# Attention scores on TensorE: the high-by-high products on 64 array rows each, the score columns over two banks, another order of steps

## The chip, the cores and the metric

The program runs on one core of a Trainium2 chip. The core has five instruction streams that wait for each other by semaphores: PE (TensorE, matrix multiply), DVE (VectorE), ACT (ScalarE), POOL (GpSimd) and SP, which here only issues DMAs. The metric is the device time of one execution in microseconds (us). The result of a matrix multiply goes to PSUM, which has 8 banks of 512 fp32 numbers in each of 128 partitions; everything else lies in SBUF.

## The reference

```python
def _attn_ref(q, k, v):                  # q, k, v: (2, 8, 576, 64) fp32
    scores = (1 / sqrt(64)) * matmul(q, k.transpose(0, 1, 3, 2))
    kth = np.partition(scores, -32, axis=-1)[..., -32:-31]
    scores = np.where(scores >= kth, scores, -1e9)
    attn = exp(scores - max(scores)); attn /= attn.sum(-1) + 1e-9
    return matmul(attn, v)

def _moe_ref(x, domain_probs, w1, w2):   # x: (1152, 512); w1: (4, 512, 1024); w2: (4, 1024, 512)
    p = domain_probs / (domain_probs.sum(-1, keepdims=True) + 1e-9)
    for e in range(4):
        out += p[:, e:e + 1] * (np.maximum(x @ w1[e], 0) @ w2[e])
```

The attention output of the 8 heads of one sequence position, side by side, is a row of x; every row goes through all four experts.

## The kernel before

**Tiles and units.** The 1152 positions are cut into ten tiles: for each of the two batches four of 128 positions and one of 64. The first tile in the program is a 64-row one (batch 0), computed in fp32; the last is the other 64-row one. A unit is one head of a 128-row tile, or a pair of heads of a 64-row tile. There are 72 units: 4, then 64 of full width (8 tiles by 8 heads), then 4.

**Numbers in two halves.** Outside the first tile every fp32 operand of a matrix multiply is split into two fp16 numbers, hi and lo. `split` does it: ACT scales, ACT writes hi, and POOL (mode "a") or DVE (mode "d") subtracts to get lo. Keys `kt[h]`, values `vt[h]`, queries, the weights of the experts, the attention weights and the hidden layer are all held so. A key tile `kt[h]` has 128 partitions: the 64 dimensions of one half, then the 64 of the other; it is made by one transposing DMA. For the queries there are two tiles: `ta` (name `qa` in rows) with the hi half on partitions 0 to 63 and lo on 64 to 127, and `tb` (`qb`) with the halves swapped.

**A unit's steps.** `emit_qk` computes scores of 128 positions by 576 keys into a PSUM tile `ps0` (two of them, each two banks). Eight DVE passes of `topk_op` (MAX8 and MATCH_REPLACE8, four rounds) find the 32 largest; ACT takes the exponential (`emit_exp`), `emit_mask` sets what is below the 32nd to zero (on DVE, or on ACT and POOL, by a letter of `MASKS`), `emit_a` splits it, `emit_at` transposes it by DMA, `emit_av` multiplies by the values on PE.

**Scores of a full unit before.** For each half of the keys (288 columns, one bank each) PE multiplies `ta` by the key tile and then `tb` by it, both with all 128 array rows: hi by hi and lo by lo, then lo by hi and hi by lo. Four matmuls of 288 columns.

```python
for j, src in enumerate((ta, tb)):
    PE.matmul(ps[:, 0:288], lhsT=src[:, x, :],
              rhs=kt[x].rearrange("p c n -> p (c n)")[:, ks], start=(j == 0), stop=(j == 1))
```

**The experts.** When the 8 units of a tile are done, its x is split and transposed (`xt`), and `m1` (three products of hi and lo, 128 columns each for a full tile), `h_hi`, `h_lo`, `m2` (512 columns each) and `evac` run for each expert and half. The eight weight arrays are split in the first fifth of the program (`w_split`, modes `W_MODE`).

**Order.** Each engine runs its instructions in program order. The order of all steps, and of the parts of a step between its `yield`s, is a table of numbers (`ISSUE`), one entry per step. Letters in strings (`H_LO`, `MASKS`, `NB`, `X_LO`, `W_MODE`, `EVAC`, `KV1`, `V0`) say for each step which engine does it.

Of the kernel before, what the change touches and what calls it, by code (L numbers as in the profile page):

```python
# [7 lines left out]
F32 = mybir.dt.float32  # L8
# [10 lines left out]
NEG = -3.0e38  # L19
# [24 lines left out]
H_LO = ('ddpp', 'ppppppdp', 'pdpdppdp', 'ppppppdp', 'pppppppp', 'pppppppp', 'pppppppp', 'pppppppp', 'pppppppp', 'pppp')  # L44

MASKS = 'ddddddddddddddddddddrrrrrrrrrrrrrrdrrrrrrrddrdrrrrrrrrrrrrrrrrrrrrrrrrrr'
NB = 'aaaapdpdddapaaaapdpdddddddpdddapppdaappaappaappaaaaapppaapaapaapppaappaa'

X_LO = 'pppdpppppp'
Q_LO = 'pppppppppp'  # L50

W_MODE = 'aaaaaaaaadaaaaaaaaaaaaaaaaadaaaa'

EVAC = ('dddp', 'dppp', 'ddpd', 'dddp', 'dppp', 'dpdp', 'dddd', 'dddd', 'dddd', 'dddd')
KV1 = dict(k='aadaaaaa', v='aaaaaaaa')
# [5 lines left out]
V0 = 'aaaaaaaa'  # L61
# [169 lines left out]
def attn_moe_kernel(tc, q, k, v, probs, w1, w2, out):  # L231
# [56 lines left out]
    with tc.manual_schedule(engines={getattr(mybir.EngineType, x) for x in MANUAL}):  # L288
# [74 lines left out]
        def prep_q(t, steps):  # L363
# [43 lines left out]
            at(steps[2], q_lo)  # L407
            at(steps[3], q_swap)

        def split(hi, lo, raw, s, mode):  # L410
            if mode == "a":
                ACT.activation(raw, raw, AF.Copy, scale=s)
            yield
# [782 lines left out]
```

## Time and profile before

| what | value |
|---|---|
| runs (3), median, lowest to highest | 553.38 us, 552.89 to 556.65 us |
| the profiled execution | 551.35 us |
| its span, first to last instruction | 549.5 us |
| mean granted TensorE clock | 0.961 |
| busy: PE, DVE, ACT, POOL | 507.8, 438.1, 372.3, 365.0 us |

The profile is of one execution; 1.85 us of it lie outside the span, and it is 2.03 us under the median of the three runs. A PE row's duration is that of one matmul from its start until its last result, and the matmuls overlap; so what a matmul costs PE is read from the distance between the starts of two rows, not from their durations. In the names of PE rows, 128\*128 or 64\*128 is how many array rows by array columns the matmul uses.

### The profile page before, as it was taken

The numbers are of one execution on the slowest core, as the hardware profiler recorded it, in microseconds if no ns is written. First come the engines' busy times: TensorE is split into PE (matmuls) and PEld (weight loads), VectorE is DVE, ScalarE is ACT, GpSimd is POOL, SyncE is SP. The second block draws the span as 40 slices with busy tenths as digits, with TensorE's granted clock in tenths as the row PEclk, the third lists the DMA queues.
The fourth block names the chain that finished last, engine by engine and source line by source line (L and its number), as shares of the span: only waits on it lengthen the run. The fifth ranks groups of instructions, "written<-read, shape, count | busy, mean of one in ns | idle before, by whom it ended". The sixth has DMA issues, their size and how long they took to land. (4 is left out here: it accounts for less than half of the span.)

```text
span 549.5 us, 16260 instructions
## 1 busy us (share of the span) xinstructions
PE 507.8 (92%) x6666; PEld 381.6 (69%) x6666; DVE 438.1 (80%) x961; ACT 372.3 (68%) x643; POOL 365.0 (66%) x410
## 2 busy tenths in 40 slices
PE   4987564889999999999999999999999999999996
PEld 2666463577777668687777678777767778676684
DVE  2899999999999999999999989999998676600101
ACT  2899999988656867787968577757766465433121
POOL 0379999989667766676979686877768273643220
PEclk9778787899999999999999999999999999999999
DMA  7999897551561362547544453362143221201100
GB/s 180 364 267 280 211 242 218 131 88 29 102 130 42 78 141 60 107 108 143 113 88 108 77 110 67 94 94 56 42 78 70 63 46 45 63 21 23 32 4 30
DMA packets 142699, 58.35 MB, mean 106 GB/s; under 512 B 130081, under 2 KB 134305, under 8 KB 142625
## 3 DMA queue, kind: packets, MB, share of 16 engines
q1 hardware_dynamic: 139200, 54.43, 43.8%
q10 hardware_dynamic: 3424, 2.88, 1.7%
q8 instruction: 52, 0.85, 0.7%
q14 instruction: 23, 0.18, 0.1%
HBM read 25.45 MB, written 2.36 MB: 51 GB/s over the span
## 5 line engine op out<-in xcount | busy, mean ns | idle before, releaser
L883 PE MATMUL m<-xt,w 128*128 128x128 f16 (+1 forms) x1280 | 200.1, 215 | 0.0
L924 PE MATMUL m<-w,h 128*128 128x512 f16 (+1 forms) x960 | 199.2, 384 | 0.0
L881 PE MATMUL m<-xt,w 128*128 128x128 f16 (+1 forms) x1120 | 178.4, 215 | 0.0
L882 PE MATMUL m<-xt,w 128*128 128x128 f16 (+1 forms) x1120 | 178.4, 215 | 0.0
L655 DVE MAX8 m<-w 128x8 f32<-128x576 f32 x216 | 161.1, 753 | 3.0
L924 PEld LDWEIGHTS <-h 128*128 128x128 f16 (+1 forms) x960 | 83.8, 102 | 89.6 <-issue 3.4
L906 POOL TENSOR_TENSOR h<-hf,h 128x512 f16<-128x512 f32 x65 | 75.3, 1159 | 75.0 <-ACT hf L899 74.2
L883 PEld LDWEIGHTS <-w 128*128 128x128 f16 x1280 | 123.8, 99 | 0.0
L881 PEld LDWEIGHTS <-w 128*128 128x128 f16 x1120 | 108.2, 98 | 3.9 <-issue 1.7
L882 PEld LDWEIGHTS <-w 128*128 128x128 f16 x1120 | 108.0, 98 | 2.3 <-issue 0.3
L659 DVE MATCH_REPLACE8 w<-m,w 128x576 f32<-128x576 f32 x144 | 106.8, 742 | 0.0
L699 ACT ACTIVATE w<-ps,nb,es 128x576 f32<-128x576 f32 x68 | 56.4, 829 | 46.8 <-DVE m L655 39.7
L726 POOL TENSOR_TENSOR a<-w,a 128x512 f16<-128x512 f32 x68 | 78.9, 1161 | 12.4 <-ACT a L724 8.4
L716 POOL TENSOR_TENSOR w<-w,d 128x576 f32<-128x576 f32 x48 | 61.4, 1281 | 36.0 <-ACT d L713 27.9
L892 ACT ACTIVATE h<-m 128x512 f16<-128x512 f32 x72 | 42.5, 591 | 53.7 <-PE m L883 48.0
L655 DVE MAX8 m<-ps 128x8 f32<-128x576 f32 x72 | 54.6, 759 | 24.7 <-PE ps L598 11.2
L948 DVE SCALAR_TENSOR_TENSOR o<-m,pniw,o 128x512 f32<-128x512 f32 (+1 forms) x17 | 12.7, 746 | 65.9 <-PE m L924 51.7
L724 ACT ACTIVATE a<-w 128x576 f16<-128x576 f32 x68 | 46.1, 680 | 15.8 <-POOL w L716 11.6
L642 PE MATMUL ps<-kt,qa 128*128 128x288 f16 x128 | 35.7, 298 | 19.8 <-DVE w L706 18.2
L657 DVE MATCH_REPLACE8 w<-m,ps 128x576 f32<-128x576 f32 x72 | 53.8, 747 | 0.0
L899 ACT ACTIVATE hf<-m 128x512 f32<-128x512 f32 x65 | 38.6, 594 | 7.0 <-POOL h L906 6.0
L764 PEld LDWEIGHTS <-at 128*128 128x128 f16 (+1 forms) x1008 | 36.6, 100 | 7.5 <-issue 1.7
(160 smaller groups left out, 786.0 us busy)
## 6 DMA issues: line engine op xcount, KB each, us to landing
w<-in_moe_w_dram SPq DMA_DIRECT2D x16, 1024.0 KB, 7.9
qraw<-in_q_dram SPq DMA_DIRECT2D x8, 256.0 KB, 3.1
qb<-qa SPq DMA_DIRECT2D x16, 128.0 KB, 2.4
out_dram<-o ACTq DMA_DIRECT2D x8, 256.0 KB, 2.2
at<-a SPq DMA_TRANSPOSE x68, 2.9
vraw<-in_v_dram SPq DMA_DIRECT2D x2, 512.0 KB, 8.2
nraw<-in_v_dram SPq DMA_DIRECT2D x4, 256.0 KB, 2.9
kraw<-in_k_dram SPq DMA_DIRECT2D x4, 256.0 KB, 2.8
```

The lines of the kernel that those rows point to most:

```text
L655: DVE.max(m, s_t[u] if r == 0 else w_t[u])
L657: DVE.match_replace(rows2(w_t[u]), m, s_t[u], NEG)
L659: DVE.match_replace(w_t[u], m, w_t[u], NEG)
L699: ACT.activation(rows2(w_t[u]), s_t[u], AF.Exp, bias=nb, scale=es)
L716: POOL.tensor_tensor(w, w, g, op=OP.mult)
L724: ACT.activation(a[:, 0:576], w, AF.Copy)
L726: POOL.tensor_tensor(a[:, 640:1152], w[:, 0:512], a[:, 0:512], op=OP.subtract)
L881: PE.matmul(o, lhsT=HI[e, 0, c][:, fc], rhs=xs(0, c), start=(c == 0), stop=False)
L882: PE.matmul(o, lhsT=HI[e, 0, c][:, fc], rhs=xs(1, c), start=False, stop=False)
L883: PE.matmul(o, lhsT=LO[e, 0, c][:, fc], rhs=xs(0, c), start=False, stop=(c == 3))
L906: POOL.tensor_tensor(h[:, 1], hf, h[:, 0], op=OP.subtract)
L924: PE.matmul(y[z * 64:z * 64 + M, :], lhsT=h_t[es, qd][:, p // 2, h0:h0 + M], rhs=w, start=(fc == 0 and p == 0), stop=(fc == 7 and p == 2))
```

## The change

For the 64 full units, the hi by hi product now uses 64 array rows: one matmul on rows 0 to 63 (from `ta`) for keys 0 to 255, one on rows 64 to 127 (from `tb`) for keys 256 to 575. For this the key tile holds hi on partitions 0 to 63 for the first two chunks of 128 keys, and on 64 to 127 for the other three. Then two matmuls with all 128 rows add lo by hi and hi by lo, `tb` for the first keys and `ta` for the others. The lo by lo product is left out. A unit still has four matmuls, now of 256, 320, 256 and 320 columns. The 576 score columns lie side by side, 256 at the end of one bank and 320 at the start of the next, so other engines read them as one run of 576 instead of two of 288. The split of the keys works on two parts where it had one (`KC`). Three loads of keys that stood in a fixed place ahead of the table now have places in it. `ISSUE` is another table, and the letters are other letters.

```diff
-H_LO = ('ddpp', 'ppppppdp', 'pdpdppdp', 'ppppppdp', 'pppppppp', ...
-MASKS = 'ddddddddddddddddddddrrrrrrrrrrrrrrrdrrrrrrrddrdrrrrrrrrrrrrrrrrrrrrrrrrr'
-X_LO = 'pppdpppppp'
+H_LO = ('pddd', 'ppppppdp', 'ddppppdd', 'ppdppppp', 'pdpppdpp', ...
+MASKS = 'ddddddddddddddddddddrrrrrrrrrrrrrrrrrrrrdrrrrrrrrrrrrrrrrrrrrrrrrrrrrrrr'
+X_LO = 'pppppppppp'
...
-W_MODE = 'aaaaaaaaadaaaaaaaaaaaaaaaaadaaaa'
-EVAC = ('dddp', 'dppp', 'ddpd', 'dddp', 'dppp', 'dpdp', 'dddd', ...
-KV1 = dict(k='aadaaaaa', v='aaaaaaaa')
+W_MODE = 'daaadaaaaaaaaaaaaaaaaaaaaaaaaaaa'
+EVAC = ('ddpp', 'dpdp', 'dppd', 'dppp', 'dppd', 'dppd', 'dddd', ...
+KV1 = dict(k='aaaaaaaa', v='aaaaaaaa')
...
-V0 = 'aaaaaaaa'
+V0 = 'aaaaadda'
...
 ISSUE = [
-    (41,), (57,), (3, 5), (1, 4), (29, 30), (32, 45), (22, 28), (11,), (17, 20), (21, 23, 42, 158), (44, 59, 91, 109),
...
+        KC = slice(0, 2), slice(2, 5)
+        def k_parts(hl, lo):
+            return [hl[:, c, D:2 * D] if lo != i else hl[:, c, 0:D] for i, c in enumerate(KC)]
...
-            return ps_s.tile([128, 2, 512], F32, tag="s", name="ps0")
+            return ps_s.tile([128, 1024], F32, tag="s", name="ps0")
...
+        HALF = (slice(256, 512), slice(0, 256)), (slice(512, 832), slice(256, 576))
...
-                else:
-                    for j, src in enumerate((ta, tb)):
-                        PE.matmul(ps[:, 0:288], lhsT=src[:, x, :],
-                                  rhs=kt[x].rearrange("p c n -> p (c n)")[:, ks], start=(j == 0), stop=(j == 1))
+            kf = flat(kt[x])
+            for (o, ks), src, z in zip(HALF, (ta, tb), (slice(0, 64), slice(64, 128))):
+                PE.matmul(p[:, o], lhsT=src[z, x, :], rhs=kf[z, ks], start=True, stop=False)
+            for (o, ks), src in zip(HALF, (tb, ta)):
+                PE.matmul(p[:, o], lhsT=src[:, x, :], rhs=kf[:, ks], start=False, stop=True)
...
-        for z in range(2):
-            SP.dma_start(out=kraw0[0:64, 4, :, z, :], in_=k[0, 4 * z:4 * z + 4, 512:576, :].rearrange("h p d -> p h d"))
-        load_k0(SP, 1)
         load_k0(ACT, 2)
-        load_k0(SP, 3)
...
+        at(-200, load_k0_end)
+        at(-199, load_k0, SP, 1)
+        at(-198, load_k0, SP, 3)
```

**PE, the scores of one full unit** (the second head of a tile; `ps0` is the score tile, `kt1` its key tile, `qa` and `qb` the two query tiles; LDWEIGHTS loads the stationary operand). Before:

```order
L642 LDWEIGHTS qa_1491
L642 MATMUL ps0_2474<-kt1_132,qa_1491 128x288
L642 LDWEIGHTS qb_1608
L642 MATMUL ps0_2474<-kt1_132,qb_1608 128x288
L642 LDWEIGHTS qa_1491
L642 MATMUL ps0_2474<-kt1_132,qa_1491 128x288
```

The same unit of the change, with the last matmul ahead of it and the first behind it:

```order
L893 MATMUL m1_2453<-xt_1932,w20_127 128x128
L651 LDWEIGHTS qa_1662
L651 MATMUL ps0_2507<-kt1_132,qa_1662 128x256
L651 LDWEIGHTS qb_2246
L651 MATMUL ps0_2507<-kt1_132,qb_2246 128x320
L653 LDWEIGHTS qb_2246
L653 MATMUL ps0_2507<-kt1_132,qb_2246 128x256
L653 LDWEIGHTS qa_1662
L653 MATMUL ps0_2507<-kt1_132,qa_1662 128x320
L891 LDWEIGHTS w11_126
```

The two matmuls of line 651 use 64 array rows; what stands ahead of them and behind them uses 128, so every full unit enters that form once and leaves it once.

**PE, the start of the program** (`ident` is the identity that transposes; `kraw0` and `qraw` are the loaded keys and queries; `ps0` the first scores). Before:

```order
L579 MATMUL m1_185<-ident_111,kraw0_150 128x128 x4
L579 MATMUL m2_186<-ident_111,kraw0_150 128x64
L558 MATMUL m1_196<-ident_111,qraw_155 128x64 x4
L598 MATMUL ps0_206<-kf_201,qf_204 64x288 x4
L1022 LDWEIGHTS kraw0_150
```

In the change:

```order
L571 MATMUL m1_177<-ident_111,qraw_155 128x64 x4
L592 MATMUL m1_186<-ident_111,kraw0_150 128x128 x4
L592 MATMUL m2_187<-ident_111,kraw0_150 128x64
L609 MATMUL ps0_196<-kf_193,qf_184 64x256 x2
L609 MATMUL ps0_196<-kf_193,qf_184 64x320 x2
```

The queries are transposed ahead of the keys instead of behind them.

**PE, where the second tile's experts begin** (`xt_1938` before and `xt_1932` now is that tile's transposed x; `m1` of the first tile reads `xt_917`; `m2` of the first tile reads `h`). Before:

```order
L882 LDWEIGHTS w30_1123
L882 MATMUL m1_1836<-xt_917,w30_1123 128x64
L883 LDWEIGHTS w30_1123
L883 MATMUL m1_1836<-xt_917,w30_1123 128x64
L881 LDWEIGHTS wx0_129
L881 MATMUL m1_1940<-xt_1938,wx0_129 128x128
```

In the change:

```order
L774 MATMUL av_1901<-vt1_140,at_1653 128x65
L934 LDWEIGHTS h_1132
L934 MATMUL m2_1591<-w01_124,h_1132 64x512
L934 MATMUL m2_1591<-w11_126,h_1132 64x512
L891 LDWEIGHTS wx0_129
L891 MATMUL m1_1966<-xt_1932,wx0_129 128x128
```

The 24 matmuls of the first tile's `m2` for experts 0 and 1, second half (of which two stand here), have moved behind its `m1` of experts 2 and 3, to the place just ahead of the second tile's first `m1`.

## Rows read from the trace of the kernel before

**Rows 1.** Page, part 1: busy us, share of span, instructions.

```profile
PE 507.8 (92%) x6666; PEld 381.6 (69%) x6666; DVE 438.1 (80%) x961; ACT 372.3 (68%) x643; POOL 365.0 (66%) x410
```

**Rows 2.** Stages of the span: busy us and count by engine, granted clock, DMA.

```profile
60.00:118.00 58.00, 40.88 (x716) 32.14 (x714) 57.69 (x142) 57.03 (x78) 57.30 (x47) 0.85 0.74 163
118.00:121.50 3.50, 1.19 (x23) 1.12 (x20) 3.50 (x4) 3.19 (x5) 3.50 (x4) 0.98 0.48 132
121.50:125.00 3.50, 3.50 (x35) 3.44 (x33) 3.46 (x5) 1.86 (x2) 1.19 (x2) 0.53 0.37 84
140.00:440.00 300.00, 298.69 (x3753) 225.66 (x3752) 278.65 (x593) 213.69 (x391) 214.28 (x262) 1.00 0.44 89
440.00:545.00 105.00, 104.56 (x1517) 75.30 (x1515) 33.25 (x65) 38.92 (x67) 43.12 (x46) 1.00 0.14 33
```

**Rows 3.** Waits of PE, 118 to 545 us: total, times, longest.

```profile
PE m L881 <- DMA xt<-xhl: 2.3, 1, 2.3
PE ps L642 <- ACT d L709: 1.3, 2, 0.7
```

**Rows 4.** Full units' score matmuls (line 642) before and after 118 us.

```profile
0.00:118.00 118.00, 10.88 (x52) 0.84 0.86 224
118.00:545.00 427.00, 33.39 (x204) 1.00 0.36 74
```

**Rows 5.** Timeline, PE, a full unit's scores at 395 us: start, duration, instruction.

```profile
394.74 0.59 PE L924 MATMUL m<-w,h 128*128 128x512 f16 x2
395.18 0.29 PE L642 MATMUL ps<-kt,qa 128*128 128x288 f16 x1
...
395.54 0.29 PE L642 MATMUL ps<-kt,qb 128*128 128x288 f16 x1
395.67 0.22 PE L881 MATMUL m<-xt,w 128*128 128x128 f16 x1
```

**Rows 6.** Timeline, PE, a 64-position unit's scores on 64 array columns, 444 us.

```profile
443.63 0.81 PE L924 MATMUL m<-w,h 128*128 128x512 f16 x3
444.38 0.31 PE L638 MATMUL ps<-kt,qa 128*64 128x288 f16 x2
444.52 0.29 PE L638 MATMUL ps<-kt,qb 128*64 128x288 f16 x2
...
444.77 0.29 PE L638 MATMUL ps<-kt,qb 128*64 128x288 f16 x2
444.99 0.23 PE L881 MATMUL m<-xt,w 128*128 128x128 f16 x1
```

**Rows 7.** Timeline, PE, fp32 transposes on 128, then 64 array rows, 14 us.

```profile
14.19 0.64 PE L579 MATMUL m<-ident,kraw 128*128 128x128 f32 x4
14.55 0.47 PE L579 MATMUL m<-ident,kraw 128*128 128x128 f32 x2
14.75 0.27 PE L579 MATMUL m<-ident,kraw 64*128 64x64 f32 x1
```

**Rows 8.** Timeline, the first scores: PE, ACT, DVE.

```profile
7.25 0.34 PE L579 MATMUL m<-ident,kraw 64*128 64x64 f32 x1 [0.78 <-DMA kraw<-in_k_dram]
8.51 2.19 PE L598 MATMUL ps<-kf,qf 64*64 64x288 f32 x8 [0.47 <-ACT qf L562]
10.74 0.77 DVE L655 MAX8 m<-ps 128x8 f32<-128x576 f32 x1 [8.95 <-PE ps L598]
```

**Rows 9.** Groups by line and form: busy, mean ns of one.

```profile
L420 DVE SCALAR_TENSOR_TENSOR w<-w,ws,w 128x1024 f16<-128x1024 f32 x1 | 2.2, 2224 | 0.0
L420 DVE SCALAR_TENSOR_TENSOR kraw<-kraw,kps,kt 128x320 f16<-128x320 f32 x1 | 0.5, 545 | 0.0
L573 ACT ACTIVATE kf<-m 128x64 f32<-128x64 f32 x4 | 0.9, 220 | 0.5 <-PE m L579 0.5
L728 POOL TENSOR_TENSOR a<-w,a 128x64 f16<-128x64 f32 x68 | 22.4, 331 | 0.1
```

More of the change, by code (lines that the diff above doesn't have):

```diff
@@ L43 @@
 MANUAL = ('PE', 'DVE', 'Activation', 'Pool', 'SP')
-H_LO = ('ddpp', 'ppppppdp', 'pdpdppdp', 'ppppppdp', 'pppppppp', 'pppppppp', 'pppppppp', 'pppppppp', 'pppppppp', 'pppp')
-MASKS = 'ddddddddddddddddddddrrrrrrrrrrrrrrdrrrrrrrddrdrrrrrrrrrrrrrrrrrrrrrrrrrr'
-NB = 'aaaapdpdddapaaaapdpdddddddpdddapppdaappaappaappaaaaapppaapaapaapppaappaa'
-X_LO = 'pppdpppppp'
+H_LO = ('pddd', 'ppppppdp', 'ddppppdd', 'ppdppppp', 'pdpppdpp', 'pppppppd', 'pppppppp', 'pppppppp', 'pdpppppp', 'pppp')
+MASKS = 'ddddddddddddddddddddrrrrrrrrrrrrrrrrrrrrdrrrrrrrrrrrrrrrrrrrrrrrrrrrrrrr'
+NB = 'aaaaadpadaddaddaddpddddddadpppadapppaappapaaapapaappaaaaaaapapappapaaaap'
+X_LO = 'pppppppppp'
 Q_LO = 'pppppppppp'
-W_MODE = 'aaaaaaaaadaaaaaaaaaaaaaaaaadaaaa'
-EVAC = ('dddp', 'dppp', 'ddpd', 'dddp', 'dppp', 'dpdp', 'dddd', 'dddd', 'dddd', 'dddd')
-KV1 = dict(k='aadaaaaa', v='aaaaaaaa')
+W_MODE = 'daaadaaaaaaaaaaaaaaaaaaaaaaaaaaa'
+EVAC = ('ddpp', 'dpdp', 'dppd', 'dppp', 'dppd', 'dppd', 'dddd', 'dddd', 'dddd', 'dddd')
+KV1 = dict(k='aaaaaaaa', v='aaaaaaaa')
 F32E = ()
@@ L408, in prep_q, with split @@
             at(steps[3], q_swap)
-        def split(hi, lo, raw, s, mode):
+        def split(hi, lo, raw, s, mode, parts=(slice(None),)):
             if mode == "a":
@@ L414, in split @@
             hi = hi()
-            ACT.activation(hi, raw, AF.Copy, scale=1.0 if mode == "a" else s)
+            for i, c in enumerate(parts):
+                ACT.activation(hi[i] if len(parts) > 1 else hi, raw[:, c], AF.Copy, scale=1.0 if mode == "a" else s)
             yield
-            if mode == "a":
-                POOL.tensor_tensor(lo, raw, hi, op=OP.subtract)
-            else:
-                DVE.scalar_tensor_tensor(lo, raw, s, hi, op0=OP.mult, op1=OP.subtract)
+            for i, c in enumerate(parts):
+                l, g = (lo[i], hi[i]) if len(parts) > 1 else (lo, hi)
+                if mode == "a":
+                    POOL.tensor_tensor(l, raw[:, c], g, op=OP.subtract)
+                else:
+                    DVE.scalar_tensor_tensor(l, raw[:, c], s, g, op0=OP.mult, op1=OP.subtract)
+        KC = slice(0, 2), slice(2, 5)
+        def k_parts(hl, lo):
+            return [hl[:, c, D:2 * D] if lo != i else hl[:, c, 0:D] for i, c in enumerate(KC)]
         def flat(ap):
@@ L446, in finish @@
                 hl = raw(h).bitcast(F16)
-                tmp = kt[h].rearrange("p c n -> p (c n)")[:, 0:320].rearrange("p (c d) -> p c d", d=D)
-                yield from split(lambda: tmp, hl[:, :, 0:D], raw(h), st["s"][:, hs.index(h):hs.index(h) + 1], mode[h])
+                t0 = kt[h][:, 0:2, :]
+                t1 = flat(kt[h])[:, 256:448].rearrange("p (c d) -> p c d", d=D)
+                yield from split(lambda: [t0[:, :, 0:D], t1], [t0[:, :, D:2 * D], hl[:, 2:5, 0:D]], raw(h),
+                                 st["s"][:, hs.index(h):hs.index(h) + 1], mode[h], KC)
                 yield
-                ACT.activation(hl[:, :, D:2 * D], tmp, AF.Copy)
+                ACT.activation(hl[:, 0:2, :], t0, AF.Copy)
+                ACT.activation(hl[:, 2:5, D:2 * D], t1, AF.Copy)
                 yield
@@ L550, in attn_moe_kernel @@
         s_t, w_t, m_t, a_t, at_t, av_t = {}, {}, {}, {}, {}, {}
-        HS = S // 2
         qF, kF = [None], {}
@@ L585, in scores @@
         def scores():
-            return ps_s.tile([128, 2, 512], F32, tag="s", name="ps0")
-        def rows2(w):
-            return w.rearrange("p (t n) -> p t n", t=2)
+            return ps_s.tile([128, 1024], F32, tag="s", name="ps0")
+        HALF = (slice(256, 512), slice(0, 256)), (slice(512, 832), slice(256, 576))
         def emit_qk_whole(u, x):
             p = scores()
-            s_t[u] = p[:, :, 0:HS]
-            for hf in range(2):
-                ps = p[:, hf, :]
+            s_t[u] = p[:, 256:832]
+            for o, ks in HALF:
                 for z in (slice(0, 64), slice(64, 128)):
-                    PE.matmul(ps[z, 0:288], lhsT=qF[0][z, x * 64:x * 64 + 64], rhs=kF[x][z, hf * 288:hf * 288 + 288],
-                              start=True, stop=True)
+                    PE.matmul(p[z, o], lhsT=qF[0][z, x * 64:x * 64 + 64], rhs=kF[x][z, ks], start=True, stop=True)
         def emit_a_whole(u):
@@ L630, in emit_qk @@
             p = scores()
-            s_t[u] = p[:, :, 0:HS]
-            for hf in range(2):
-                ps = p[:, hf, :]
-                ks = slice(hf * 288, hf * 288 + 288)
-                if t[2] == 64:
+            s_t[u] = p[:, 256:832]
+            if t[2] == 64:
+                for o, ks in HALF:
                     for j, src in enumerate((ta, tb)):
                         for z, h in enumerate(hpair(x)):
-                            PE.matmul(ps[z * 64:z * 64 + 64, 0:288], lhsT=src[:, x, z * 64:z * 64 + 64],
-                                      rhs=kt[h].rearrange("p c n -> p (c n)")[:, ks], start=(j == 0), stop=(j == 1))
-                else:
-                    for j, src in enumerate((ta, tb)):
-                        PE.matmul(ps[:, 0:288], lhsT=src[:, x, :],
-                                  rhs=kt[x].rearrange("p c n -> p (c n)")[:, ks], start=(j == 0), stop=(j == 1))
+                            PE.matmul(p[z * 64:z * 64 + 64, o], lhsT=src[:, x, z * 64:z * 64 + 64],
+                                      rhs=flat(kt[h])[:, ks], start=(j == 0), stop=(j == 1))
+                return
+            kf = flat(kt[x])
[3 more added lines that the diff above has]
+                PE.matmul(p[:, o], lhsT=src[:, x, :], rhs=kf[:, ks], start=False, stop=True)
         def topk_op(u, o):
@@ L656, in topk_op @@
             elif r == 0:
-                DVE.match_replace(rows2(w_t[u]), m, s_t[u], NEG)
+                DVE.match_replace(w_t[u], m, s_t[u], NEG)
             else:
@@ L698, in emit_exp @@
             es, nb = eb_t.pop(u)
-            ACT.activation(rows2(w_t[u]), s_t[u], AF.Exp, bias=nb, scale=es)
+            ACT.activation(w_t[u], s_t[u], AF.Exp, bias=nb, scale=es)
         def emit_mask(u):
             thr = m_t[u][:, 31:32]
-            w = rows2(w_t[u])
+            w = w_t[u]
             s = s_t.pop(u)
@@ L708, in emit_mask @@
                 d = sp_.tile([128, S], F32, tag="s", name="d")
-                ACT.activation(rows2(d), s, AF.Relu, bias=thr, scale=-1.0)
+                ACT.activation(d, s, AF.Relu, bias=thr, scale=-1.0)
             yield
             if MASKS[u] == "r":
-                g = d.bitcast(F16).rearrange("p (t n) -> p t n", t=2)[:, :, 0:HS]
-                ACT.activation(g, rows2(d), AF.Exp, scale=-1.0e18)
+                g = d.bitcast(F16)[:, 0:S]
+                ACT.activation(g, d, AF.Exp, scale=-1.0e18)
             yield
@@ L979, in attn_moe_kernel, with load_k0_end @@
         load_q(tiles[0])
-        for z in range(2):
-            SP.dma_start(out=kraw0[0:64, 4, :, z, :], in_=k[0, 4 * z:4 * z + 4, 512:576, :].rearrange("h p d -> p h d"))
-        load_k0(SP, 1)
         load_k0(ACT, 2)
-        load_k0(SP, 3)
+        def load_k0_end():
+            for z in range(2):
+                SP.dma_start(out=kraw0[0:64, 4, :, z, :],
+                             in_=k[0, 4 * z:4 * z + 4, 512:576, :].rearrange("h p d -> p h d"))
+        at(-200, load_k0_end)
+        at(-199, load_k0, SP, 1)
+        at(-198, load_k0, SP, 3)
         def load_v0(h0):
@@ L1045, in kv_finish @@
                 hl = khl0[:, h]
-                yield from split(lambda: hl[:, :, D:2 * D], hl[:, :, 0:D], kraw0[:, :, h % 4, h // 4], st["s"], K0[h])
+                yield from split(lambda: k_parts(hl, 0), k_parts(hl, 1), kraw0[:, :, h % 4, h // 4], st["s"], K0[h], KC)
                 yield
```

320 rows, old and new, of the table ISSUE are left out of this document.

## The prediction

> **What bounds the kernel now.** I read the shares by engine first: PE is busy 92% of the span [rows 1]. That average hides two regimes, so the stages come next [rows 2]. From 60 to 118 us DVE, ACT and POOL are all busy for 57.0 to 57.7 of 58 us and PE for 40.9: there the first units and the splits of the weights set the pace. From 140 to 440 us PE is busy 298.7 of 300 us while DVE has 278.7 and ACT and POOL some 214, and from 440 to 545 us PE has 104.6 of 105 with the others nearly idle. A busy PE need not be PE at its rate, so the waits of PE were read as the third view: from 118 to 545 us it waits 2.3 us in one place, for the second tile's transposed x, and 1.3 us in two others [rows 3]. So for 427 us PE issues matmuls without a gap, and whatever a matmul there costs or saves goes into the end of the program one for one. Ahead of 118 us it does not: there PE waits anyway. The full units' scores have 52 matmuls before 118 us and 204 after it [rows 4]; at four a unit these are 13 and 51 units. The 51 decide.
>
> **The score matmuls, what they save.** Among matmuls that use the whole array, four of 288 columns start at 395.18 us and the next work starts at 395.67 [rows 5]: 0.49 us, or 0.1225 us for 288 columns. The changed unit has 256, 320, 256 and 320 columns, the same 1152. Only if the two 64-row matmuls run beside each other does PE stream 320 columns for both, and 256 fall out: 256/288 x 0.1225 = 0.109 us a unit. No row of before has two 64-row matmuls over the same columns. The nearest are pairs that use 64 columns each: the four pairs of a 64-position unit start at 444.38, 444.52 and so on to 444.77 [rows 6], so two matmuls of 288 columns take the time of one. I take the overlap as given and keep its absence as a rival.
>
> **What they cost.** The same rows show what it costs to enter and leave such a form. Three 512-column matmuls start from 443.63; at 288 columns in 0.1225 us one takes 0.217, so the next was due at 443.63 + 3 x 0.217 = 444.28. The first pair starts at 444.38: 0.10 us late. The second pair follows after 0.14 instead of 0.12: 0.02. The last pair starts at 444.77 and the whole-array matmul behind it at 444.99, 0.22 later where 0.12 would do: 0.10. One visit to the form costs 0.22 us as these rounded rows have it, 0.20 to 0.22 in all. That is for 64 columns; for 64 rows there is one clean place [rows 7]. Four fp32 transposes on the whole array start within 0.64 - 0.27 = 0.37 us of 14.19, 0.12 us apart. The fourth starts at 14.55, and the one on 64 rows at 14.75: 0.20 us, so at least 0.08 us late. Leaving is not clean there, because the next transpose is of another chain of keys. I take 0.21 for a visit, from the 64-column row, whose matmuls are of the same kind. Lower end: 0.08 us each way, 0.16. Upper end: 0.22, and no overlap.
>
> So a full unit changes by 0.21 - 0.109 = +0.10 us, between +0.05 and +0.11 with overlap, and by +0.21 without. Over 51 units: **+5.1 us**, between +2.6 and +5.6, and +10.7 without overlap. Nothing hides it: PE has 3.6 us of waits in the whole region, and 2.3 of them are for x. The 13 early units pay it beside DVE and are free.
>
> **The start.** Before, the queries' transposes stand behind a key chunk that PE waits 0.78 us for, and the first scores wait 0.47 us more for the copied queries [rows 8]. Now they stand ahead of the keys, and the copy is done in time. The keys' second copy (0.22 us, [rows 9]) follows the chunk's transpose, which ends at 7.59, so the scores can start at about 7.85 in place of 8.51: DVE begins 0.65 us earlier. Against that, DVE has two weight splits of 2.2 us and two value splits of 0.55 us within the first 118 us [rows 9], where it had one weight split there and one behind; one `h_lo` of like size goes the other way. DVE's sum up to the second half of the second tile's x is larger by 0 to 2.6 us, by where these steps stand, while POOL loses as much. Since all three engines are full there [rows 2], I put the start at +0.1 us, ends -0.7 and +2.
>
> **The clock.** After the wait for x, during which PE was busy 1.2 of 3.5 us, the granted clock is 0.53 for 3.5 us, nearly its lower level of 1.2 of 2.4 GHz, although PE is full [rows 2]: 3.5 x 0.47 = 1.6 us of PE's time, in the region that decides. The change puts 24 matmuls of 512 columns, in pairs, just ahead of that place: 12 x 0.217 = 2.6 us of work where PE stood. If PE no longer stands, the clock may stay up. That is even odds: -0.8 us, ends -1.6 and 0. The wait itself isn't saved by this, since the same matmuls ran earlier before, in gaps.
>
> **Edits that cost nothing.** The key splits have 24 more ACT instructions and 16 more POOL ones, each a short one of at most 0.22 and 0.33 us [rows 9], so at most 5.3 us on each engine; three masks move from DVE to ACT and POOL, six `h_lo` the other way, and two evacuations. In the region that decides ACT and POOL have some 86 us free in 300 and DVE 21 [rows 2]; that covers all of it. Reading 576 columns in one run instead of two of 288 changes no count of elements. The three freed loads of keys stand in SP's queue where they stood, behind the first queries and ahead of the weights. The last units and the last tile's experts stand in nearly the same order, so the tail keeps its length.
>
> **The sum.** +5.1 + 0.1 - 0.8 = +4.4 us. The profiled execution took 551.35 us (span 549.5 and 1.85 around it); one like it would take 555.75. The median of the three runs is 2.03 us higher, and so I say 553.38 + 4.4 = **557.8 us**. A difference of about 1% (5.5 us) is what a measurement of this kernel can tell from none; this forecast lies under it.
>
> **Rivals.**
> *Entering the form is free.* If a 64-row matmul needs no pause among whole-array ones, each unit saves the whole 0.109 us: 51 x 0.109 = 5.6, with the clock and the start 6.3, so 547.1 us, and faster. Against it are rows 6 and 7: each change of form there has its 0.08 to 0.10 us, the one of 64 rows too. For it: two of those three are changes of columns, not rows, and the third is a single place. The Trainium skill ("TensorE: Matmul & The Clock Gate", the part on packing small matmuls) describes this outcome: a group of packed tiles lasts one matmul plus some 4 ns a tile, with weights loaded beside matmuls on other rows, and no price for entering. By that rule this rival's time holds; rows 6 agree with the few ns inside a pair and not with a free entry.
> *The halves don't run beside each other.* Then PE streams all 1152 columns and pays the visits as well: +10.7 - 0.8 + 0.1 = +10.0, 563.4 us, slower. It decides if the second 64-row matmul starts 0.11 us behind the first instead of some ns. For it: no such pair is in the trace. Against it: rows 6, and the two halves write different banks. The Trainium skill ("TensorEngine Tiling (Array Packing)", Gotcha 1) says that row tiles cannot write the same PSUM bank at once; by it these two may overlap. No row here shows it.
> *The new order wins back what PE loses.* If the region in which PE is full begins 4 us earlier, because its work starts earlier beside the splits, the result is 553.4 us, no change. For it: PE stands idle for 17 of 58 us before 118 us [rows 2], and every step was placed anew. Against it: the amount of DVE's work that x of the second tile needs has not shrunk.
>
> **Chances and range.** Forecast 0.56, free entry 0.16, no overlap 0.12, won back by the order 0.12, and 0.04 for what I have not thought of. The forecast's own ends are 553.7 (+2.6 - 0.7 - 1.6 = +0.3) and 561.0 (+5.6 + 2.0). The range reaches from 547.0, about the middle of the free entry, to 562.0, just under the middle of the third case: it leaves out some 0.08 on each side. Faster by over 1% is under 547.85: most of the free entry, 0.13. Slower by over 1% is over 558.9: the third case and about 0.16 of the forecast's 0.56, together 0.28. The rest, 0.59, is within 1%.
>
> **What would show it.** Where a full unit follows whole-array work, the first 64-row matmul starts about 0.10 us later than the columns ahead of it need; the second starts within 0.02 us of it; and the next whole-array matmul starts about 0.23 us behind (320 columns are 0.136, and the exit 0.10). From first start to the next work a unit takes about 0.50 us instead of 0.49, with 0.10 more ahead of it. PE's waits from 118 us on stay at 2 to 4 us, the granted clock just behind the second tile's first `m1` tells of the 1.6 us, and DVE's first MAX8 starts near 10.1 instead of 10.74. The prediction is wrong if units come without the pauses, if the pair comes one after the other, or if PE fills at another time than near 120 us.

## The result, and the profile after

The changed kernel takes 559.76 us in the median of four runs (559.21 to 560.12), the kernel before 553.23 us (552.89 to 556.65): a ratio of 1.0103, with an interval of 1.0062 to 1.0144. That is 6.5 us slower. In a second set of runs the ratio was 1.0132 (1.0098 to 1.0165), and the kernel before against itself gave 0.9998 (0.9974 to 1.0022), so the loss is real and lies at the edge of 1%. The forecast was 557.8 us. The two profiled executions differ by more than the medians, 559.7 us (span 557.9) against 551.35, because the kernel before's lies 1.9 us under its median.

The page's first part and the stages, which answer to [rows 1, 2] (busy us and count by engine, granted clock, DMA):

```profile
PE 517.1 (93%) x6666; PEld 379.8 (68%) x6666; DVE 435.9 (78%) x962; ACT 378.2 (68%) x671; POOL 365.6 (66%) x422
```

```profile
60.00:118.00 58.00, 38.32 (x608) 31.33 (x608) 56.09 (x139) 54.69 (x73) 54.34 (x45) 0.78 0.77 163
118.00:121.50 3.50, 2.73 (x92) 2.60 (x88) 3.46 (x11) 3.15 (x5) 3.44 (x3) 1.00 0.53 118
121.50:125.00 3.50, 3.50 (x42) 1.95 (x40) 3.50 (x9) 3.50 (x6) 3.50 (x3) 1.00 0.33 75
125.00:140.00 15.00, 14.54 (x197) 10.67 (x196) 14.90 (x37) 13.62 (x21) 14.13 (x11) 1.00 0.21 37
140.00:440.00 300.00, 299.32 (x3713) 217.38 (x3711) 276.21 (x586) 218.72 (x411) 219.74 (x274) 1.00 0.45 90
```

Two things differ. From 60 to 118 us DVE has 1.9 us of idle time where it had 0.3, and ACT and POOL 3.3 and 3.7 us where they had 1.0 and 0.7: the region in which they set the pace is no longer full. And the granted clock from 121.5 to 125 us is 1.00 where it was 0.53; it stays at 1.00 behind that.

PE's waits from 118 us on, answering to [rows 3], and the second tile's first `m1`, in the kernel before and now:

```profile
PE ps L651 <- DVE w L716: 0.8, 1, 0.8
PE m L891 <- DVE h L912: 0.5, 1, 0.5
PE m L891 <- DMA xt<-xhl: 0.4, 1, 0.4
PE ps L651 <- ACT d L719: 0.2, 1, 0.2
```

```profile
120.41 0.22 PE L881 MATMUL m<-xt,wx 128*128 128x128 f16 x1 [2.31 <-DMA xt<-xhl]
125.67 0.23 PE L891 MATMUL m<-xt,wx 128*128 128x128 f16 x1 [0.46 <-DVE h L912]
```

From this matmul on PE is nearly full in both. So the difference between the two traces splits at this row: the start is 5.3 us longer, and what follows it, 432.2 us in place of 429.1 (the "rest" below), is 3.1 us longer.

A full unit among whole-array work (timeline, PE), answering to [rows 5]:

```profile
395.79 1.04 PE L774 MATMUL av<-vt,at 128*128 128x65 f16 x28
396.77 0.28 PE L651 MATMUL ps<-kt,qa 64*128 64x256 f16 x1
396.77 0.31 PE L651 MATMUL ps<-kt,qb 64*128 64x320 f16 x1
397.01 0.28 PE L653 MATMUL ps<-kt,qb 128*128 128x256 f16 x1
397.13 0.30 PE L653 MATMUL ps<-kt,qa 128*128 128x320 f16 x1
397.27 2.10 PE L934 MATMUL m<-w,h 128*128 128x512 f16 x9
```

The two 64-row matmuls start in the same hundredth: they do run beside each other. The last of the 28 matmuls of 65 columns starts at 396.64 and needs 0.03 us, so the pair comes 0.10 us late; the next matmul is 0.24 us behind it. First start to next work is 0.50 us, and 0.10 more stands ahead: each number is that of the prediction.

The weight loads say more about these two pauses than the prediction did. In the kernel before, the second matmul of the unit of [rows 5] starts at 395.30 us, and its weight load at 395.18, with the matmul ahead of it. In the unit above, the load for the matmul at 396.77 starts at 396.77, and the load for the one at 397.01 at 397.01. At both edges of all 51 units the load starts with its own matmul. A load lasts 0.09 to 0.10 us, which is the size of a pause. So a load that no earlier matmul covers would account for it; no run here tells that from another cause of the same size.

The start. DVE's first MAX8 comes 0.35 us earlier than in [rows 8] (forecast 0.65; the last key chunk is transposed at 7.89 us, not at 7.25), and DVE's waits from 10 us on are these:

```profile
10.39 0.77 DVE L665 MAX8 m<-ps 128x8 f32<-128x576 f32 x1 [8.60 <-PE ps L609]
```

```profile
DVE m L665 <- PE ps L609: 10.0, 3, 8.6
DVE m L518 <- PE m L512: 3.6, 1, 3.6
DVE m L665 <- PE ps L653: 1.8, 2, 1.4
DVE wpt L282 <- PE m L521: 1.3, 1, 1.3
```

Line 512 is the sum of squares (the gram) of the third weight matrix, `w_gram` for (0, 1), line 518 its diagonal on DVE, line 521 its total on PE. The kernel before (lines 498 and 507) waits 0.7 and 0.4 us for all such:

```profile
DVE m L504 <- PE m L498: 0.7, 1, 0.7
DVE wpt L281 <- PE m L507: 0.4, 2, 0.2
```

On PE the new order has an attention product of the first tile (lines 629 and 632, unit 2) ahead of that gram and one (unit 3) ahead of its total:

```profile
42.32 1.12 PE L629 MATMUL av<-vraw,at 128*64 128x64 f32 x16
...
45.03 3.59 PE L512 MATMUL m<-w 128*128 128x128 bf16 x32
48.56 1.12 PE L629 MATMUL av<-vraw,at 128*64 128x64 f32 x16
...
51.28 0.59 PE L521 MATMUL m<-gd,ones 128*128 128x1 f32 x2
```

```profile
43.74 1.41 DVE L665 MAX8 m<-w 128x8 f32<-128x576 f32 x2
48.74 0.30 DVE L518 SCALAR_TENSOR_TENSOR m<-m,ident 128x128 f32<-128x128 f32 x1 [3.59 <-PE m L512]
```

DVE comes to the diagonal at 45.15 us, when the gram has just begun, and stands in order, with top-k work queued behind. PE has no gap there, but it is slow:

```profile
40.00:44.00 4.00, 3.82 (x37) 2.88 (x37) 4.00 (x11) 4.00 (x9) 2.71 (x5) 0.60 1.05 394
44.00:48.00 4.00, 4.00 (x48) 3.97 (x47) 1.15 (x2) 3.06 (x4) 2.24 (x4) 0.50 0.92 200
48.00:52.00 4.00, 4.00 (x51) 3.54 (x50) 1.94 (x7) 1.78 (x3) 1.27 (x1) 0.50 0.77 191
```

The granted clock of these three stretches is 0.60, 0.50 and 0.50, where 0.50 is the lower level of 1.2 GHz. In the kernel before it is 0.86, 0.72 and 1.00, and its gram takes 2.42 us, not 3.59:

```profile
45.32 2.42 PE L498 MATMUL m<-w 128*128 128x128 bf16 x32
```

```profile
40.00:44.00 4.00, 2.25 (x32) 1.92 (x31) 3.68 (x10) 4.00 (x7) 3.34 (x5) 0.86 0.40 66
44.00:48.00 4.00, 4.00 (x49) 3.33 (x49) 4.00 (x9) 3.99 (x7) 3.92 (x4) 0.72 0.98 311
48.00:52.00 4.00, 4.00 (x90) 3.57 (x85) 3.45 (x11) 3.71 (x6) 3.42 (x3) 1.00 1.15 309
```

### The profile page after: what moved, and what is told of

It reads as the page before. It is cut to its first block, busy times and chain, and to the rows that moved or that the text cites. A ratio compares the mean times of both kernels' runs of the same rounds, so it can differ in the third digit from the quotient of the medians.

```text
span 557.9 us, 16250 instructions
## 1 busy us (share of the span) xinstructions
PE 517.1 (93%) x6666; PEld 379.8 (68%) x6666; DVE 435.9 (78%) x962; ACT 378.2 (68%) x671; POOL 365.6 (66%) x422
## 4 chain that ended last, share of the span: by engine, by line
PE 71%; DVE 18%; POOL 4%; DMA 3%; issue 3%; ACT 1%; SPq 0%; POOLq 0%; DVEq 0%
PE m L934 29%; PE m L891 9%; PE m L893 9%; PE m L892 9%; DVE m L665 7%; PE av L774 4%; DVE w L669 4%; PE ps L653 3%; DVE w L667 2%; PE ps L651 2%; DVE w L716 2%; DMA at<-a 1%; PE ps L609 1%; DMA xt<-xhl 1%; DMA kraw<-in_k_dram 1%
## 5 line engine op out<-in xcount | busy, mean ns | idle before, releaser
L934 PE MATMUL m<-w,h 128*128 128x512 f16 (+1 forms) x960 | 196.7, 379 | 0.0
L916 POOL TENSOR_TENSOR h<-hf,h 128x512 f16<-128x512 f32 x59 | 68.5, 1161 | 66.6 <-ACT hf L909 66.6
L726 POOL TENSOR_TENSOR w<-w,d 128x576 f32<-128x576 f32 x51 | 65.4, 1283 | 28.2 <-ACT d L723 28.1
L958 DVE SCALAR_TENSOR_TENSOR o<-m,pniw,o 128x512 f32<-128x512 f32 (+1 forms) x15 | 11.2, 745 | 63.8 <-PE m L934 49.8
L774 PEld LDWEIGHTS <-at 128*128 128x128 f16 (+1 forms) x1008 | 38.2, 101 | 13.7 <-DMA at<-a 6.6
L774 PE MATMUL av<-vt,at 128*128 128x65 f16 (+1 forms) x1008 | 41.1, 196 | 6.1 <-DVE w L716 4.6
L719 ACT ACTIVATE d<-ps,m 128x576 f32<-128x576 f32 x51 | 37.5, 737 | 3.8 <-DMA at<-a 2.2
```

The costliest lines, as they stand in the source:

```text
L726: POOL.tensor_tensor(w, w, g, op=OP.mult)
L774: PE.matmul(o, lhsT=att[:, blk, ps], rhs=r, start=(i == 0), stop=(i == len(seq) - 1))
L916: POOL.tensor_tensor(h[:, 1], hf, h[:, 0], op=OP.subtract)
L934: PE.matmul(y[z * 64:z * 64 + M, :], lhsT=h_t[es, qd][:, p // 2, h0:h0 + M], rhs=w, start=(fc == 0 and p == 0), stop=(fc == 7 and p == 2))
```

## The experiments

Theory A was that form and order each have a cost of their own; theory B that the form costs all, C that the order does. All ratios are to the kernel before in the same set of runs; e1 to e4 are one set, the two kernels again with e5 and e6 a second, e7 to e9 a third.

**e1, the changed kernel without the 64-row form.**

```diff
-            for (o, ks), src, z in zip(HALF, (ta, tb), (slice(0, 64), slice(64, 128))):
-                PE.matmul(p[:, o], lhsT=src[z, x, :], rhs=kf[z, ks], start=True, stop=False)
-            for (o, ks), src in zip(HALF, (tb, ta)):
-                PE.matmul(p[:, o], lhsT=src[:, x, :], rhs=kf[:, ks], start=False, stop=True)
+            for o, ks in HALF:
+                for j, src in enumerate((ta, tb)):
+                    PE.matmul(p[:, o], lhsT=src[:, x, :], rhs=kf[:, ks], start=(j == 0), stop=(j == 1))
```

> The changed kernel with its four score products of a full unit again on all 128 rows of the array (key layout, order of steps, banks and everything else as changed). Theory A, the form and the new order each cost their own part: the 51 full units in which TensorE never waits give back 0.10 us each, so 559.8 - 5.1 = 554.7 us, a unit of 0.49 us with no 0.095 ahead of it, and the second tile's first m1 still starts near 125.6 us. Theory B, the form alone costs all, in the start too: 551 to 553 us, with that m1 back near 120.4 us. Theory C, the form is free and the new order costs all: 559.8 us.

Measured: 554.81 us, ratio 1.0066 (1.0038 to 1.0093). The unit is as the kernel before's (the changed lines are one fewer, so later line numbers are one lower):

```profile
394.77 0.27 PE L652 MATMUL ps<-kt,qa 128*128 128x256 f16 x1
...
395.12 0.30 PE L652 MATMUL ps<-kt,qb 128*128 128x320 f16 x1
395.26 2.75 PE L933 MATMUL m<-w,h 128*128 128x512 f16 x12
```

0.49 us. The `m1` stays late, at 126.62 us, so B falls; the rest is 429.0 us in place of 432.2, so C falls. It gives back 3.3 us of the 5.1: behind that `m1` PE now waits 1.5 us where the changed kernel waits 0.6, and the cause of another 0.9 us stays open.

**e2, the kernel before with the 64-row form** (key layout, columns and form of the changed kernel; order, letters and key loads of before).

> The other way round: the kernel before, with its order, letters and first key loads, but with the keys laid out by parts, the scores over 256 and 320 columns and the high by high products on 64 rows each. Theory A: 51 units at +0.10 us on the kernel before, 553.2 + 5.1 = 558.3 us, the second tile's first m1 within 1 us of 120.4 us. Theory B: 559.8 us, that m1 near 125.6 us. Theory C: 553.2 us.

Measured: 556.75 us, ratio 1.0087 (1.0052 to 1.0122), `m1` at 122.27, rest 433.2. So the form costs time without the new order, 0.87% and near A's 5.1 us, and C falls. But `m1` is 1.9 us later than in the kernel before, where A allowed 1 us.

**e3, two visits a unit.**

```diff
+            for (o, ks), hi, lo, z in zip(HALF, (ta, tb), (tb, ta), (slice(0, 64), slice(64, 128))):
+                PE.matmul(p[:, o], lhsT=hi[z, x, :], rhs=kf[z, ks], start=True, stop=False)
+                PE.matmul(p[:, o], lhsT=lo[:, x, :], rhs=kf[:, ks], start=False, stop=True)
```

> The changed kernel with the same four products of a full unit in another order: each half's 64-row product and then its product on all rows, so that a unit enters and leaves the 64-row form twice and the two 64-row products never lie beside each other. Theory A, each entry and each exit costs about 0.10 us: a unit takes 0.095 + 0.107 + 0.105 + 0.107 + 0.095 + 0.133 + 0.105 + 0.136 = 0.88 us in place of 0.59, 51 x 0.29 = +15 us, 574.8 us. Theory D, a visit has no price of its own and only the lost overlap (0.11 us a unit) counts: +5.6 us, 565.4 us.

Measured: 576.16 us, ratio 1.0441 (1.0388 to 1.0493); its rest is 447.3 us, 15.0 more than the changed kernel's, as A has it, and D falls. The unit:

```profile
397.26 0.28 PE L651 MATMUL ps<-kt,qa 64*128 64x256 f16 x1
397.48 0.28 PE L652 MATMUL ps<-kt,qb 128*128 128x256 f16 x1
397.69 0.31 PE L651 MATMUL ps<-kt,qb 64*128 64x320 f16 x1
397.93 0.31 PE L652 MATMUL ps<-kt,qa 128*128 128x320 f16 x1
398.08 0.60 PE L773 MATMUL av<-vt,at 128*128 128x65 f16 x14
```

256 columns need 0.11 us, and from start to start it is 0.22 and 0.21: one pause of 0.10 on the way out, one on the way in.

**e4, the gram ahead of both attention products** (the places of two steps in the table of order: 167 is the attention product of unit 2, 173 that of unit 3; the gram has 169, its total 180).

```diff
-    (67,), (121,), (128,), (131, 476, 1217), (150, 160), (932,), (167,), (94,), (138,), (143,), (151, 1041, 1930),
-    (163, 172), (963,), (173,), (216, 228, 242), (246,), (262, 275), (135,), (39, 159, 170), (194,), (198, 697, 2065),
+    (67,), (121,), (128,), (131, 476, 1217), (150, 160), (932,), (180.3,), (94,), (138,), (143,), (151, 1041, 1930),
+    (163, 172), (963,), (180.6,), (216, 228, 242), (246,), (262, 275), (135,), (39, 159, 170), (194,), (198, 697, 2065),
```

> The changed kernel with one difference in TensorE's order: the attention products of the first tile's units 2 and 3 stand behind the sum of squares of the third weight matrix (its gram and its total) and not ahead of them. Theory A, the start's loss is VectorE standing 3.6 + 1.3 us for that gram and total in order: the stand falls to about 1 us, while ScalarE's scaling of the first values waits about 1.2 us longer for those products, so the second tile's first m1 comes 2 to 4 us earlier (121.6 to 123.6 us) and the time is 555.8 to 557.8 us. Theory E, VectorE's stand is covered and something else sets the end of the start: 559.8 us, that m1 at 125.6 us.

Measured: 556.77 us, ratio 1.0096 (1.0061 to 1.0131), beside 1.0103 and 1.0132 for the changed kernel in other sets; `m1` at 121.20, 4.5 us earlier. PE, and the granted clock of the same stretches:

```profile
41.66 2.82 PE L512 MATMUL m<-w 128*128 128x128 bf16 x32
45.01 0.38 PE L521 MATMUL m<-gd,ones 128*128 128x1 f32 x2 [0.53 <-DVE m L518]
45.32 0.69 PE L629 MATMUL av<-vraw,at 128*64 128x64 f32 x16
```

```profile
40.00:44.00 4.00, 4.00 (x36) 3.44 (x35) 4.00 (x9) 3.99 (x8) 2.72 (x7) 0.57 1.07 392
44.00:48.00 4.00, 3.47 (x77) 2.98 (x74) 3.87 (x11) 2.47 (x5) 2.19 (x2) 1.00 1.23 217
```

DVE no longer waits for gram or total. E falls. The trace gains more than the 2 to 4 us expected, and the clock comes back too: the gram takes 2.82 us in place of 3.59, a product's first part 0.69 in place of 1.12. The time gains less, 2 us at most.

**The changed kernel, the kernel before, and e5 and e6 in one set.** e5 is e1 and e4 at once; e6 is e2 with the four products on all rows.

> The changed kernel once more, beside the others of this set on one chip, so that the size of the single effects can be read there. Theory A (form +0.10 us a full unit, new order's start late): 1.0103 times the kernel before, and in its trace the second tile's first m1 again 4 to 6 us later than in the kernel before's. Theory F, the late start was an accident of the one profiled execution: the ratio again about 1.010, but that m1 within 2 us of 120.4 us.

> The kernel before once more, unchanged: ratio 1.000, which shows what the comparison can tell apart, and a second trace of its start. Theory A: the second tile's first m1 within 1.5 us of 120.4 us. Theory F: as late as in the changed kernel, 123 us or more.

> Both single changes at once on the changed kernel: the four products of a full unit on all rows, and the third weight matrix's gram and total ahead of the first tile's attention products of units 2 and 3. Theory A, the two losses are separate and add up: start as with the gram first (m1 near 121.2 us) and the rest as with full rows (429.0 us), a span of 550.2 us, 552 us on a chip where the changed kernel takes 559.8, so within 0.5 per cent of the kernel before. Theory G, one loss hides the other: 555 us or more, a ratio of 1.006 or above.

> The kernel before with its order, letters and key loads, the keys laid out by parts and the scores over 256 and 320 columns, but all four products on all rows: what is left of the change when form and order are taken out. Theory A: these parts cost and bring nothing, a ratio of 1.000 (0.997 to 1.003), rest 429 us. Theory H, the split of the keys in two parts (one instruction more a head on two engines) delays the start: second tile's first m1 1 to 2 us later (as the 122.3 us of the old order with the 64-row form), a ratio of 1.002 to 1.004.

Measured: the changed kernel 559.12 us, 1.0132; before 551.2, 0.9998 (0.9974 to 1.0022); e5 552.63, 1.0020 (0.9997 to 1.0042); e6 551.51, 0.9979 (0.9950 to 1.0007). The late start repeats (125.06 against 120.60), F falls; the rest of this second pair differs by only 0.9 us (432.0 against 431.1). The time of e5 is A's, so G falls: with both undone nothing is left that this comparison can tell from none. Its parts are not A's: `m1` is at 122.98 and not near 121.2, and the rest is 427.1 and not 429.0. The stand has moved to the next gram, which e4 ran in 2.01 us and e5 runs in 3.59, at a clock of 0.51:

```profile
49.57 3.59 PE L512 MATMUL m<-w 128*128 128x128 bf16 x32
```

```profile
DVE m L518 <- PE m L512: 2.0, 1, 2.0
```

For layout, columns and key splits e6 shows no cost, H falls (`m1` at 119.11).

**e7, only unit 2's product behind the gram** (167 becomes 169.5).

> The changed kernel with the attention product of unit 2 alone put behind the third weight matrix's gram on TensorE; that of unit 3 stays ahead of the gram's total. Theory A (VectorE stands in order, first for the gram, then for its total): the first stand falls from 3.6 us to 1 us or less, but the total still comes behind both products, near 51.5 us, so that the second stand grows from 1.3 to about 3.5 us; the sum and the second tile's first m1 stay within 1 us, ratio 1.011 to 1.013. Theory J, the gram's own lateness is what counts: the ratio falls to 1.008 to 1.010, as with both products behind it, m1 2 us or more earlier.

Measured: 557.01 us, 1.0086 (1.0054 to 1.0119), `m1` at 122.61. Here A's number was wrong: it counted the products at the lower clock. With the gram first the clock is 1.00 from 44 us on, the total comes at 47.85 and not near 51.5, and the second stand is 1.7 us. J's numbers came out.

**e8, PE's order as changed, DVE's two steps later in DVE's queue** ((178, 180) becomes (187.3, 187.6), and 193 becomes 200.5).

> The changed kernel with TensorE's instructions in the changed order, but VectorE's two steps on that gram put later in its own queue: the diagonal behind two more top-k operations, the total behind a weight split, a mask and two top-k operations more. Theory A: VectorE's work goes on while TensorE is as late as before; the two stands of 4.9 us shrink to about 2 us plus a wait for the mask's input of under 1 us, m1 1.5 to 3 us earlier, ratio 1.008 to 1.010. Theory K, it is TensorE's lateness itself (the attention products, the gram, what stands behind them), not VectorE's standing: m1 near 125 us as before, ratio 1.011 to 1.013.

Measured: 558.38 us, 1.0105 (1.0068 to 1.0142); `m1` at 123.70, and the stand for the gram 1.6 us with none for the total, as A has it. The ratio lies between A's range and K's, and the gain in time is not resolved from the changed kernel's 1.0103 and 1.0132.

**e9, the kernel before with unit 2's product ahead of the gram** (176 becomes 174.5).

> The kernel before with the one difference in TensorE's order turned round: the attention product of unit 2 ahead of the third weight matrix's gram, as in the changed kernel. Theory A (the loss needs both, TensorE's order and VectorE reaching the diagonal early): VectorE reaches it at 48.8 us there, the gram ends at 49.2 to 50.5 us in place of 47.7, a stand of 0.4 to 1.7 us, the total's wait 0 to 1 us; ratio 1.000 to 1.004. Theory L, a product ahead of the gram costs what it costs in the changed kernel, by the clock or otherwise: 3 us or more, ratio 1.006 or above.

Measured: 552.59 us, 1.0007 (0.9977 to 1.0036), so the time is A's. The trace is nearer to L: DVE's waits and the clock are

```profile
DVE m L504 <- PE m L498: 2.8, 1, 2.8
```

```profile
44.00:48.00 4.00, 4.00 (x53) 3.62 (x53) 3.75 (x10) 3.70 (x7) 3.89 (x4) 0.50 0.99 324
48.00:52.00 4.00, 4.00 (x52) 3.62 (x51) 1.42 (x4) 3.47 (x6) 3.40 (x3) 0.55 1.13 336
```

With the one product moved, the lower clock and a stand of 2.8 us come into the kernel before as well; but other waits of DVE shrink there, and the sum grows by 1.4 us only.

All profiled executions in one table (us): the second tile's first `m1`, DVE's waits from 10 to 126 us summed, their difference, and what follows that `m1`.

| kernel | order | rows of high by high | m1 | DVE's waits | difference | rest |
|---|---|---|---|---|---|---|
| before | old | 128 | 120.41 | 13.2 | 107.2 | 429.1 |
| before again | old | 128 | 120.60 | 13.5 | 107.1 | 431.1 |
| e6 | old | 128 | 119.11 | 11.9 | 107.2 | 431.2 |
| e9 | old, one moved | 128 | 121.85 | 14.6 | 107.3 | 428.9 |
| e2 | old | 64 | 122.27 | 15.0 | 107.3 | 433.2 |
| changed | new | 64 | 125.67 | 16.7 | 109.0 | 432.2 |
| changed again | new | 64 | 125.06 | 15.9 | 109.2 | 432.0 |
| e1 | new | 128 | 126.62 | 17.7 | 108.9 | 429.0 |
| e3 | new | 64, two visits | 127.32 | 18.3 | 109.0 | 447.3 |
| e8 | new, DVE later | 64 | 123.70 | 14.4 | 109.3 | 432.7 |
| e7 | new, one moved | 64 | 122.61 | 13.2 | 109.4 | 432.6 |
| e4 | new, two moved | 64 | 121.20 | 11.6 | 109.6 | 433.1 |
| e5 | new, two moved | 128 | 122.98 | 14.4 | 108.6 | 427.1 |

The start is DVE's work plus its waits, in every kernel: the difference is 107.1 to 107.3 in the old order and 108.6 to 109.6 in the new one. The rest is 427.1 to 431.2 us without the form and 432.0 to 433.2 with one visit a unit. Each line is one execution, and executions of one kernel differ by several us (the kernel before: 548.5 to 555.0 us in the second set), so 1 or 2 us between two lines may not be the kernels'.

Two things that are not the form lie in the rest. One is PE's waits behind that `m1`, 0.4 to 3.2 us. The other is the lower clock just behind it, about 1.6 us in four kernels of the old order (before, before again, e2, e6). Without both, the rest is 426.2 to 427.5 us without the form (mean 426.7) and 431.1 to 432.1 with one visit a unit (mean 431.7): 5.0 us apart.

In time, each loss by itself is clear of the kernel before: e2, the form without the new order, 1.0087 (1.0052 to 1.0122), and e1, the new order and letters without the form, 1.0066 (1.0038 to 1.0093).

## Why the prediction was right, and where it was not

**The score matmuls: right, saving and price.** The pair overlaps, the entry is 0.10 us late, the exit costs 0.10. Over 51 units +5.1 us stands. e1 and e2 undo it and do it alone; e3 doubles the visits and pays +15.0 us. The rest as it stands shows 3.3 us (e1) or 3.2 (432.6 and 429.4 in the mean, without e3), within the ends given, +2.6 to +5.6; without waits and lower clock it shows 5.0. That the 13 early units pay nothing is not settled: with the form, `m1` is 3.2 us later in the old order (e2, e6) and 1.0 and 1.8 us earlier in the new one (changed and e1, e4 and e5).

**The start: the step that failed.** It was put at +0.1 us with an upper end of +2, and it is +5.3 in the first pair of traces and +4.5 in the second. The working summed DVE's work up to the second tile's x and, but for the first scores, took the waits as unchanged. The sum was good: "larger by 0 to 2.6" is 109.1 against 107.2, +1.9. What was left out is the waits, 13.2 before and 16.7 after: +3.5. The stands for gram and total alone, 4.9 us where it had 1.1, are +3.8. By its own last sign the prediction was wrong here: PE fills at 125.67 us, not near 120. The sentence that the three engines are full there was read from 60 to 118 us; the stand is at 45 to 52, which [rows 2] do not show. That an order moves two small products ahead of a gram could be read from the program; that DVE would reach the diagonal at 45.15 and PE the gram at 45.03 and at half clock could not be read from it. That these products matter in the new order is shown in the traces (e4, e7: `m1` 4.5 and 3.1 us earlier than in the first trace of the changed kernel); in time neither is clear of the changed kernel.

**The clock: right in kind, the term mis-sized.** Even odds gave -0.8; the granted clock is 1.00 behind the second tile's first `m1` too, where the kernel before had 0.53 for 3.5 us, so the whole -1.6 came. PE was 2.7 of 3.5 us busy from 118 us, where it had been 1.2. That the moved matmuls are the reason is not shown: in e9 they stand where they stood, PE was busy for 1.7 of these 3.5 us, and the clock from 121.5 to 125 us was 1.00 as well.

**The sum.** On the profiled pair: +5.1 (form), -1.6 (clock), -0.7 for PE's waits behind that `m1` (0.6 where it had 1.3) and +5.3 (start) are +8.1, and 8.35 was measured. The forecast had +4.4: the start was off by +5.2, clock and waits by -1.5 in the other direction. Medians differ by 6.5, and 559.76 is inside the range and even inside the forecast's own ends (up to 561.0), although the start passed its end of +2 by 3.3 us. That is partly luck: errors of opposite sign, and medians that differ by 1.9 us less than the profiled pair.

**The rivals.** "Entering the form is free" is refuted by the pauses in the unit's rows, by e2 and by e3. The Trainium skill ("TensorE: Matmul & The Clock Gate", the part on packing small matmuls) gives a group of packed tiles one matmul's time and a few ns a tile: the trace agrees inside the pair, whose matmuls both start at 396.77 us. It shows 0.10 us at each edge beside that. "The halves don't run beside each other" is refuted by these two starts. "The new order wins back what PE loses" came out with the other sign: the order moved the start by 5 us, but later. (By its own sum, +4.4 - 4, that rival's time was 553.8 us, not 553.4.)

**What stays open.** What sets the clock from 40 to 52 us. With a product ahead of the gram it was granted 0.50 to 0.59 from 44 to 48 us in all six executions (the changed kernel twice, e1, e3, e8, e9); with the gram first 1.00 (e4, e5, e7), 0.83 (e6), 0.72 and 0.64 (the kernel before twice), but 0.50 in e2. In e5 the lower clock came later, 0.51 from 48 to 52 us. So the order goes with it in most executions, and is not all. How much of the start's loss shows in the time is known only roughly, from different sets: e4 and e7 have 1.0096 and 1.0086 beside 1.0103 and 1.0132 for the changed kernel, at most 2 to 2.5 us, where their traces have 2.5 to 4.5.

## What to carry to other kernels

Where a full engine changes the form of its matmuls for a short group, count the pauses at both edges first: here 0.20 us a visit against 0.11 us saved, so by these two numbers, as an estimate, the form would pay only if one visit carried about twice the work. When instructions are put in a new order, adding up each engine's work is not enough: for each engine that sets the pace, take the steps at which it waits in order for another, and find what stands ahead of the awaited step there and at what clock it runs. Split the span at the point from which one engine is full, and check both parts by themselves: errors of opposite sign, +5.2 and -1.5 us here, make a forecast look better than its working.

## What was not expected of the hardware

PE was busy for 11.8 of 12 us from 40 to 52 us and was granted 0.60, 0.50 and 0.50; in e4 and e7, the same work in another order, it was granted 1.00 from 44 to 52 us while it was busy for 10.9 and 10.7 us of the 12. In the kernel before, the move of one product ahead of the gram (e9) went with a fall from 0.72 and 1.00 to 0.50 and 0.55. So in these stretches the granted clock did not follow PE's busy time, part of which the lower clock itself makes. And changing from 128 rows to 64 and back has the price that changing columns has in [rows 6]: 0.10 us each way.
